# Batch 0's token-major k made by TensorE transposes, weights in 4 KB rows, constants in two loads, new order tables

## The chip, the cores and the metric

One core of a Trainium2 chip runs the whole program. The metric is device time in microseconds (us). Three executions of the kernel before took 506.56, 507.03 and 507.12 us; the median, 507.03, is the time before.

## The reference

Per batch (8 of them, 576 tokens) a retention layer feeds a gated MLP with spatial mixing:

```python
scores = (q @ k.T) / sqrt(64)                    # 8 heads of 64
D[t, s] = gamma_h ** (t - s) if t >= s else 0    # gamma_h = 1 - 2 ** (-5 - h)
x = concat_heads((scores * D) @ v)               # 576 x 512
h = relu(x @ w_in)                               # w_in 512 x 1024
u, v = h[:, :512], h[:, 512:]
v_n = (v - mean(v)) / sqrt(var(v) + 1e-6)        # over the 512 features
v_s = w_spatial @ v_n + b_spatial[:, None]       # over the 576 tokens
out = (u * v_s) @ w_out                          # w_out 512 x 512
```

Weights come in as float64, all other inputs as float32.

## The kernel before

**Tiling.** A batch is four chunks of 128 tokens and a tail of 64. The retention is computed chunk by chunk as small fp32 products of 64x64: scores inside a chunk, a running state (k times v, decayed) from chunk to chunk, and the state's share of the output. They are written to two PSUM tiles called `r` in the listings. Everything after the retention is done in wide products: each fp32 value is split into a high and a low part (`split_quarter`, `weight`, `spatial`), and a product is three products of parts (`mm3`), written to four PSUM banks called `m`. The projection by the u half of w_in and the output projection of batches 2 to 7 use sums and differences of quarter blocks (`made_weight`, `summed_quarter`, `product_chain`), seven block products in place of eight.

**The state of a chunk.** `update` multiplies the token-major k (tile `kn`) by v (`vv`), so k must stand in two layouts: feature-major for the scores (the second half of tile `qk`) and token-major for the state. Before, both come by DMA (`load`), and `prep_k` scales the token-major one by a decay per token. `state_chain` holds the update, the half state `sh`, the decays `dec` and the new state `st`. `burst_chain` adds the state's share to the output in two halves (`carried`, each 16 small products for a chunk), between which ScalarE writes a 1x2 copy (`turned`, called the turn copy below); then come `values` and the evacuation.

**Weights.** `fetch` loads 512 KB of a float64 weight as 32-bit words, and `weight` turns them into a high and a low part: GpSimd or VectorE masks the sign word (the tiles `lent_vn` and `f`), ScalarE moves it to a bank (m<-lent_slot), VectorE puts the fraction in (two operations), ScalarE casts the high part (win<-lent_vn), and GpSimd or VectorE subtracts for the low part (win<-lent_vn,win). In the listings `lent_slot` holds the v half of w_in, `raw` the u half.

**The order.** All engines run in program order. Each step is a generator, and a table of tokens says whose next stage is issued: `g.1.2` is the next stage of the scores of batch 1, chunk 2; `b` is a burst, `p` a state chain, `k` and `q` the scaling of k and q, `w` a weight, `d` the loads of a chunk, `W` a block product, `K`, `R`, `Z`, `Y` the splits of its right sides; letters behind the numbers choose the engine. `ORDER` holds the start and batches 0 and 1, `STEADY` is run four times for one batch after another, `LAST` ends the program, and the digits of `BANKS` give the PSUM bank of each product in turn. A token `z` issues a product on a zeroed tile (`wsp`, 128x512) whose result is not used; the text calls it a spin:

```python
def spin(name, n):
    ps = bank()
    for i in range(n):
        pe.matmul(ps, idle[:, :P], idle, start=True, stop=True)
```

All loads are issued by SyncE (SP) in the order of the tokens, and land through 16 DMA engines.

Of the kernel before, what the change touches and what calls it, by code (L numbers as in the profile page):

```python
# [18 lines left out]
P = 128  # L19
# [24 lines left out]
    d.0.0 d.0.0 c.a q.0.0.p d.0.0 z.22.1 k.0.0.v z.4.1 z.0.1 z.12.1 z.26.1 z.36.1 z.27.1 z.17.1 z.18.1 z.29.1  # L44
    z.10.1 z.6.1 z.13.1 z.16.1 g.0.0 p.0.0.va p.0.0.va z.34.1 b.0.0 z.40.1 z.21.1 z.1.1 g.0.0 D.1.0 D.1.1 p.0.0.va
    p.0.0.va w.1.0.vp w.1.0.vp w.1.0.vp w.1.1.vp b.0.0 w.1.1.vp d.0.1 d.0.1 d.0.1 p.0.0.va z.35.1 b.0.0 b.0.0
    z.14.1 z.8.1 z.3.1 z.2.1 z.30.1 b.0.0 z.20.1 z.5.1 z.39.1 k.0.1.p g.0.1 q.0.1.p D.1.2 D.1.3 d.0.2 w.1.2.pp
    w.1.1.vp w.1.0.vp b.0.0 w.1.1.vp w.1.1.vp p.0.1.aa p.0.1.aa b.0.1 w.1.3.vp p.0.1.aa b.0.1 w.1.0.vp w.1.2.pp
    w.1.3.vp w.1.1.vp w.1.0.vp g.0.1 z.25.1 z.9.1 z.41.1 z.33.1 z.31.1 z.7.1 z.28.1 b.0.1 b.0.1 z.24.1 z.38.1
    z.37.1 v.0.0 z.32.1 b.0.1 D.0.1 T.0 D.0.0 w.1.2.pp w.1.3.vp w.1.3.vp w.1.2.pp p.0.1.aa k.0.2.a w.1.2.pp g.0.2  # L50
    p.0.2.aa q.0.2.p w.1.2.pp w.1.3.vp p.0.1.aa b.0.1 w.0.1.vp g.0.2 p.0.2.aa w.0.0.vp w.0.0.vp p.0.2.aa p.0.2.aa
    w.1.3.vp z.19.1 v.0.0 z.23.1 v.0.0 b.0.2 b.0.2 v.0.0 w.0.1.vp d.0.3 q.0.3.p t.0.p t.0.p b.0.2 d.1.0 b.0.2 v.0.0
    p.0.2.aa b.0.2 w.0.1.vp w.0.1.vp c.t D.0.2 S d.1.0 d.1.0 d.1.1 S S S w.0.2.pp k.1.0.p m q.1.0.p g.0.3 k.0.3.a
    v.0.1 z.42.1 z.11.1 v.0.1 z.15.1 v.0.1 p.0.3.ap w.0.0.vp b.0.2 w.0.0.vp v.0.0 v.0.2 v.0.2 v.0.1 t.0.p p.0.3.ap
    v.0.0 w.0.2.pp s.0.p p.0.3.ap w.0.0.vp v.0.1 w.0.2.pp g.0.3 p.0.3.ap w.0.2.pp v.0.0 b.0.3 g.1.0 b.0.3 p.1.0.pp
# [36 lines left out]
"""
STEADY = """
    W.a.0.1.C W.a.0.0.A W.a.0.0.C W.a.0.0.A W.a.0.1.A T.b W.a.0.0.A k.b.1.v W.a.0.0.C b.b.0 g.b.1 b.b.0 W.a.0.0.A
    b.b.0 W.a.0.1.A b.b.0 d.b.2 W.a.0.1.C p.b.1.vp q.b.1.p d.b.2 W.a.0.0.A d.b.2 g.b.1 p.b.1.vp W.a.0.0.B W.a.0.0.A
    p.b.1.vp b.b.0 W.a.0.0.E W.a.0.0.B v.a.4 p.b.1.vp W.a.0.0.E W.a.0.0.B v.a.0.v W.a.0.1.A W.a.0.0.B v.a.0.v
    k.b.2.p v.a.2.a W.a.0.1.B W.a.0.1.A v.a.2.a v.a.4 v.a.0.v p.b.1.vp W.a.0.1.E v.a.0.v v.a.2.a W.a.0.1.A v.a.2.a
    b.b.1 W.a.0.1.A g.b.2 W.a.0.1.B b.b.1 v.a.0.v p.b.2.pp b.b.1 v.a.0.v b.b.1 d.b.3 W.a.0.1.E W.a.0.1.B d.b.3
    p.b.2.pp v.a.1.a d.b.3 g.b.2 p.b.2.pp W.a.1.0.A v.a.1.a q.b.2.p v.a.4 W.a.1.0.A W.a.0.1.B v.a.4 b.b.1 p.b.2.pp
    W.a.1.0.A v.a.4 p.b.2.pp W.a.1.0.C v.a.4 W.a.1.0.A v.a.1.a W.a.1.0.A W.a.1.0.C k.b.3.p v.a.4 v.a.1.a W.a.1.1.C  # L100
    v.a.2.a v.a.4 W.a.1.1.A v.a.1.a v.a.3.p v.a.2.a b.b.2 g.b.3 v.a.1.a b.b.2 v.a.4 t.b.p p.b.3.vp v.a.4 t.b.p
    W.a.1.0.A b.b.2 q.b.3.p W.a.1.1.A b.b.2 d.c.0 W.a.1.1.C W.a.1.0.B d.c.0 b.b.2 v.a.4 W.a.1.1.A W.a.1.0.B v.a.4
    v.a.3.p W.a.1.0.E W.a.1.1.A v.a.4 v.a.3.p W.a.1.0.B W.a.1.0.E v.a.3.p W.a.1.1.A W.a.1.1.B W.a.1.0.B v.a.3.p
    W.a.1.1.E v.a.3.p X.a.0.0 W.a.1.1.A W.a.1.1.B p.b.3.vp W.a.1.1.E p.b.3.vp X.a.0.2 g.b.3 t.b.p p.b.3.vp X.a.0.0
    X.a.0.1 b.b.3 X.a.0.1 g.c.0 X.a.0.2 b.b.3 b.b.3 b.b.3 d.c.1 d.c.1 X.a.1.3 e.b.v d.c.0 b.b.3 Y.a.1.v e.b.v
# [929 lines left out]
```

## Time and profile before

| | before |
|---|---|
| median of three runs | 507.03 us (506.56 to 507.12) |
| the profiled execution, its own time | 506.91 us |
| its span in the trace | 504.8 us |
| granted TensorE clock, mean | 1.00 |
| TensorE (PE) busy | 498.3 us, 99% |
| VectorE (DVE) busy | 389.2 us, 77% |
| ScalarE (ACT) busy | 259.2 us, 51% |
| GpSimd (POOL) busy | 152.5 us, 30% |
| DMA | 55.52 MB, mean 110 GB/s |

The span runs from the first to the last thing that the profiler sees; the execution's own time is 2.1 us longer. PEld is TensorE's loading of stationary operands, beside its products. An engine is busy when an instruction of it runs; the time that it waits is not counted. All three vector engines have free time on average, so what is read below is where in the span TensorE waits, and for which of them.

### The profile page before, as it was taken

Reading aid. Unit: us, or ns where it says so; the run is one execution under the profiler, and the core shown is the slowest. Engines: PE = TensorE matmul, PEld = TensorE weight load, DVE = VectorE, ACT = ScalarE, POOL = GpSimd, SP = SyncE. Lnnn points to the kernel's source line nnn. Section 1 sums busy time; section 2 is a strip of 40 time slices with the busy share of each in tenths; the row PEclk is TensorE's granted clock in tenths of the full one; section 3 lists DMA queues with packets and bytes.
Section 4 is the critical chain, followed back from the end, with each engine's and each line's share of the span. In section 5 each row is a group of like instructions: output and inputs, shape, how many; then the busy total and the mean of one; then the engine's idle time right before and its main releaser. Section 6 shows DMA issues by size and latency. Waiting matters only on the chain.

```text
span 504.8 us, 17011 instructions
## 1 busy us (share of the span) xinstructions
PE 498.3 (99%) x7335; PEld 472.8 (94%) x7335; DVE 389.2 (77%) x869; ACT 259.2 (51%) x587; POOL 152.5 (30%) x133
## 2 busy tenths in 40 slices
PE   8999999999999999999999999999999999999997
PEld 6688999999999999999999999999999999999997
DVE  3787798875899876888679786888867886788756
ACT  3788535654363642647236472446525574357513
POOL 1778733252137421335014250243303240020000
PEclk9999999999999999999999999999999999999999
DMA  8979340332426322153122442054221520011002
GB/s 283 410 260 316 113 142 3 96 112 95 121 65 189 127 66 84 57 176 94 63 79 92 150 141 80 6 162 148 72 86 41 186 91 3 1 36 59 1 2 94
DMA packets 29516, 55.52 MB, mean 110 GB/s; under 512 B 2945, under 2 KB 15361, under 8 KB 29186
## 3 DMA queue, kind: packets, MB, share of 16 engines
q1 hardware_dynamic: 29442, 54.45, 32.6%
q8 instruction: 57, 0.93, 0.8%
q14 instruction: 17, 0.14, 0.1%
HBM read 45.00 MB, written 9.44 MB: 108 GB/s over the span
## 4 chain that ended last, share of the span: by engine, by line
PE 92%; DVE 4%; DMA 3%; ACT 1%; issue 0%; SPq 0%
PE m L203 78%; PE r L203 13%; DVE u L203 2%; DMA lent_slot<-in_w_in 2%; DMA fixed_terms<-in_terms 1%; DVE slot L203 1%; ACT slot L203 1%; DVE lent_vn L203 0%; DVE m L203 0%; SPq L203 0%; DVE st L203 0%; DVE at L203 0%
## 5 line engine op out<-in xcount | busy, mean ns | idle before, releaser
L203 PE MATMUL m<-wsp,vn 128*128 128x288 f32 x768 | 113.8, 297 | 0.0
L203 PEld LDWEIGHTS m<-wsp,vn 128*128 128x128 f32 x768 | 105.7, 188 | 0.7
L203 DVE TENSOR_TENSOR u<-m,u 128x288 f32<-128x288 f32 (+1 forms) x132 | 57.2, 438 | 17.2 <-PE m L203 9.8
L203 ACT COPY u<-m 128x288 f32<-128x288 f32 (+1 forms) x92 | 34.6, 384 | 33.2 <-PE m L203 24.4
L203 PE MATMUL m<-slot,win 128*128 128x288 f32 x336 | 50.5, 296 | 0.0
L203 PEld LDWEIGHTS m<-slot,win 128*128 128x128 f32 x336 | 46.7, 188 | 0.8 <-ACT u L203 0.2
L203 DVE SCALAR_TENSOR_TENSOR u<-u,m 128x288 f32<-128x288 f32 x48 | 21.2, 451 | 25.3 <-PE m L203 25.1
L203 PE MATMUL m<-slot,wout 128*128 128x288 f32 x264 | 39.8, 296 | 0.0
L203 POOL TENSOR_TENSOR slot<-u,slot 128x576 fp32r<-128x576 f32 x7 | 10.0, 1432 | 93.2 <-ACT slot L203 93.2
L203 PEld LDWEIGHTS m<-slot,wout 128*128 128x128 f32 x264 | 36.5, 188 | 0.6 <-DVE vn L203 0.3
L203 PE MATMUL m<-win,slot 128*128 128x512 f32 (+1 forms) x168 | 37.0, 351 | 0.0
L203 ACT CAST slot<-u 128x576 fp32r<-128x576 f32 x32 | 21.5, 675 | 25.6 <-DVE u L203 25.4
L203 PEld LDWEIGHTS m<-win,slot 128*128 128x128 f32 x168 | 26.7, 188 | 4.7 <-DVE slot L203 0.4
L203 ACT CAST places<-u 128x576 fp32r<-128x576 f32 x21 | 14.2, 677 | 30.5 <-DVE u L203 30.3
L203 PE MATMUL m<-quarter,slot 128*128 128x256 f32 x216 | 29.7, 283 | 0.0
L203 ACT COPY r<-warm 1x2 f32<-1x2 f32 x32 | 4.9, 152 | 47.8 <-PE r L203 47.6
L203 DVE TENSOR_TENSOR at<-r,fixed_terms 128x512 f32<-128x512 f32 x32 | 21.9, 683 | 8.5 <-PE r L203 6.9
L203 POOL TENSOR_TENSOR kn<-kn,fixed_terms 128x512 f32<-128x512 f32 x15 | 16.1, 1075 | 39.3 <-DMA kn<-in_qkv 34.1
L203 POOL TENSOR_TENSOR places<-x,places 128x576 fp32r<-128x576 f32 x6 | 10.5, 1756 | 57.0 <-ACT places L203 55.3
L203 PE MATMUL m<-slot,part 128*128 128x288 f32 x168 | 27.3, 301 | 0.4
L203 PE MATMUL m<-wtl,vt 128*128 128x288 f32 (+1 forms) x128 | 27.4, 295 | 0.0
L203 PEld LDWEIGHTS m<-quarter,slot 128*128 128x128 f32 x216 | 26.9, 188 | 0.4
(164 smaller groups left out, 1214.4 us busy)
## 6 DMA issues: line engine op xcount, KB each, us to landing
qk<-in_qkv SPq DMA_DIRECT2D x30, 512.0 KB, 4.3
kn<-in_qkv SPq DMA_DIRECT2D x30, 256.0 KB, 4.8
vv<-in_qkv SPq DMA_DIRECT2D x30, 256.0 KB, 4.7
out<-u SPq DMA_DIRECT2D x28, 144.0 KB, 1.8
tail<-in_tails SPq DMA_DIRECT2D x8, 384.0 KB, 3.5
out<-o SPq DMA_DIRECT2D x18, 144.0 KB, 1.9
lent_slot<-in_w_in SPq DMA_DIRECT2D x4, 512.0 KB, 9.3
raw<-in_w_in SPq DMA_DIRECT2D x4, 512.0 KB, 11.2
```

The source lines that it names most:

```text
L203: ins = op(*args, **kw)
```

## The change

**Token-major k of batch 0.** Chunks 0 to 3 of batch 0 no longer load `kn`. `prep_k` has two stages for them: four transposes on TensorE (`pe.transpose`, 128x128 each, by an identity tile `eye`) from the feature-major k into a bank `m`, and the scaling out of that bank into the same tile. The chunk's array in memory is laid q, k, v, k so that chunks 2 and 3, which load in one DMA, can leave it out. Batches 1 to 7 load both as before.

**Weights in 4 KB rows.** The host lays the u half of w_in and w_out so that each 512 KB load is 128 rows of 4 KB; before, a row was four pieces of 1 KB. The v half had 4 KB rows before and keeps them.

**Constants in two loads.** `terms` is cut into the mask with the decays (128x524) and the scales of q (`qterms`, 128x256); the identity (`unit`, 128x128) is a third small load. The last rows of the spatial weights come in one load in place of two.

**The tables.** ORDER, STEADY, LAST and BANKS are laid anew: the same stages with other engines for some, in another order. A few places of it follow.

SP's queue of loads at the start, before (`in_w_in` is w_in, its v half first):

```order
L203 DMA qk_94<-in_qkv 128x1024
L203 DMA kn_95<-in_qkv 128x512
L203 DMA fixed_terms<-in_terms 128x780
L203 DMA vv_96<-in_qkv 128x512
L203 DMA lent_slot_93<-in_w_in 128x512 x2
L203 DMA qk_171<-in_qkv 128x1024
L203 DMA kn_172<-in_qkv 128x512
L203 DMA vv_173<-in_qkv 128x512
L203 DMA lent_slot_93<-in_w_in 128x512 x2
L203 DMA u<-in_qkv 128x2048
```

and now (`in_w_v` is that v half):

```order
L206 DMA qk_95<-in_qkv 128x1024
L206 DMA eye<-in_unit 128x128
L206 DMA fixed_terms<-in_terms 128x524
L206 DMA vv_97<-in_qkv 128x512
L206 DMA qk_118<-in_qkv 128x1024
L206 DMA qs<-in_qterms 128x256
L206 DMA lent_slot_94<-in_w_v 128x512
L206 DMA vv_120<-in_qkv 128x512
L206 DMA u<-in_qkv 128x1536
L206 DMA lent_slot_94<-in_w_v 128x512 x3
L206 DMA lent_wout_136<-in_qkv 128x1536
```

Chunk 1's q and k moved ahead of all weights, both chunks' `kn` loads are gone, and three of the four v weights moved behind chunk 2 (`u`).

ScalarE at the start, before:

```order
L203 CAST slot_207<-r_90 128x2x4x64
L203 CAST win_66<-lent_vn_92 128x512
L203 ACTIVATE dec_79<-sh,fixed_terms 128x64 x4
L203 COPY r_90<-warm 1x2
L203 CAST win_66<-lent_vn_92 128x512
L203 ACTIVATE m_87<-lent_slot_93 128x512
L203 ACTIVATE m_86<-lent_slot_93 128x512
L203 CAST slot_207<-r_90 128x2x4x64
L203 ACTIVATE u<-u,fixed_terms 128x64 x8
```

and now:

```order
L206 CAST slot_263<-r_91 128x2x4x64
L206 ACTIVATE dec_80<-sh,fixed_terms 128x64 x4
L206 ACTIVATE u<-m_90,fixed_terms 128x64 x8
L206 COPY r_91<-warm 1x2
L206 CAST win_67<-lent_vn_93 128x512
L206 ACTIVATE m_90<-lent_slot_94 128x512
L206 ACTIVATE dec_79<-st_76,fixed_terms 128x64 x4
L206 ACTIVATE m_87<-lent_slot_94 128x512
L206 CAST win_67<-lent_vn_93 128x512
```

The scaling of chunk 2's k (u, x8, now out of the bank `m_90`) moved ahead of the first weight's casts (win<-lent_vn), and the moves of weights 0 and 2 to their banks stand behind it.

VectorE in a steady batch, around the gating (SCALAR_TENSOR_TENSOR on `u`) and the splits behind it (u<-u is a difference of quarter blocks, slot<-u,slot and places<-u,places the low part of a quarter), before:

```order
L203 TENSOR_TENSOR slot_831<-u,slot_831 128x2x288
L203 SCALAR_TENSOR_TENSOR u<-u,m_86 128x288
L203 SCALAR_TENSOR_TENSOR u<-u,m_89 128x288
L203 TENSOR_TENSOR u<-u 128x2x288 x3
L203 TENSOR_TENSOR places_2105<-u,places_2105 128x2x288
L203 TENSOR_TENSOR slot_831<-u,slot_831 128x2x288
L203 TENSOR_TENSOR u<-u 128x2x288
L203 TENSOR_TENSOR o_1481<-m_88,o_1481 128x288
```

and now:

```order
L206 SCALAR_TENSOR_TENSOR u<-u,m_88 128x288
L206 TENSOR_TENSOR u<-u 128x2x288
L206 TENSOR_TENSOR slot_944<-u,slot_944 128x2x288
L206 TENSOR_TENSOR u<-m_90,u 128x288
L206 TENSOR_TENSOR u<-u 128x2x288
L206 SCALAR_TENSOR_TENSOR u<-u,m_87 128x288
L206 TENSOR_TENSOR slot_944<-u,slot_944 128x2x288 x2
L206 TENSOR_TENSOR xt<-r_91,xt 128x4x64
L206 TENSOR_TENSOR x_1116<-xt 128x8x32
L206 TENSOR_TENSOR u<-u 128x2x288
```

Before, three differences stand between the last gating and the next low part of `slot`; now they stand ahead of it, and two low parts follow right behind it.

The diff, with a line or two of each table:

```diff
-    d.0.0 d.0.0 c.a q.0.0.p d.0.0 z.22.1 k.0.0.v z.4.1 z.0.1 z.12.1 z.26.1 z.36.1 z.27.1 z.17.1 z.18.1 z.29.1
+    d.0.0 z.26.1 z.21.1 z.27.1 z.20.1 z.0.1 z.18.1 z.29.1 z.38.1 z.36.1 z.5.1 z.1.1 z.24.1 z.13.1 z.11.1 z.22.1 c.e
+    c.a d.0.0 d.0.1 c.q D.1.1 d.0.1 q.0.0.p m q.0.1.p d.0.2 D.1.3 D.1.0 D.1.2 d.0.3 T.0 D.0.0 k.0.0.v z.2.1 g.0.0
...
-    W.a.0.1.C W.a.0.0.A W.a.0.0.C W.a.0.0.A W.a.0.1.A T.b W.a.0.0.A k.b.1.v W.a.0.0.C b.b.0 g.b.1 b.b.0 W.a.0.0.A
+    W.a.0.1.A W.a.0.0.A T.b k.b.1.v W.a.0.0.A v.a.4 v.a.4 v.a.4 W.a.0.0.C W.a.0.0.C W.a.0.1.A W.a.0.0.A W.a.0.1.A
...
-    fixed_terms = cp.tile([P, 2 * NP * D + NP * D + H + NP], F32, name="fixed_terms")
+    fixed_terms = cp.tile([P, 2 * NP * D + H + NP], F32, name="fixed_terms")
     am = fixed_terms[:, :512].rearrange("r (i p n) -> r i p n", i=2, p=NP)
-    qs = fixed_terms[:, 512:768].rearrange("r (p n) -> r p n", p=NP)
-    kd = fixed_terms[:, 768:768 + H].rearrange("r (h n) -> r h n", n=1)
-    sd = fixed_terms[:, 768 + H:].rearrange("r (p n) -> r p n", n=1)
+    kd = fixed_terms[:, 512:512 + H].rearrange("r (h n) -> r h n", n=1)
+    sd = fixed_terms[:, 512 + H:].rearrange("r (p n) -> r p n", n=1)
+    qs = cp.tile([P, NP, D], F32, name="qs")
...
+    def eye():
+        return keep("eye", [P, P], tag="o1")
...
-            qk, kn, vv = t[:, :2], t[:, 2], t[:, 3]
+            qk, vv, kn = t[:, :2], t[:, 2], t[:, 3]
...
-            parts = (qk, qkv[b, c, :, :2]), (kn, qkv[b, c, :, 2]), (vv, qkv[b, c, :, 3])
-        else:
-            parts = (t, qkv[b, c]),
+            parts = (qk, qkv[b, c, :, :2]), (kn, qkv[b, c, :, 3]), (vv, qkv[b, c, :, 2])
+            parts = parts if b else parts[::2]
+        else:
+            parts = (t[:, :3], qkv[b, c, :, :3]),
...
-            dma(t.bitcast(U64), w_in[i * P:(i + 1) * P, DH:])
         else:
             t = keep("raw", [P, NCB * S], I32)[:, i * 1024:(i + 1) * 1024] if i < 2 else keep(f"raw{i}", [P, 1024], I32)
-            w = w_in if kind == 0 else w_out
-            dma(t.bitcast(U64).rearrange("p (a n) -> p a n", a=NCB), w[:, i * P:(i + 1) * P].rearrange("(a p) n -> p a n", p=P))
+        dma(t.bitcast(U64), (w_u, w_v, w_out)[kind][i])
...
     def prep_k(b, c, eng=po):
         kh = chunk[b, c][2].rearrange("p (h d) -> p h d", h=H)
-        scale(kh, kh, kd, eng)
+        if b:
+            scale(kh, kh, kd, eng)
+            yield
+            return
+        ps = bank()
+        for p in range(NP):
+            pe.transpose(ps[:, p * P:(p + 1) * P], chunk[b, c][1][:, p], eye())
+        yield
+        scale(kh, ps.rearrange("p (h d) -> p h d", h=H), kd, eng)
...
-        for i in range(2):
-            dma(w[i * TL:(i + 1) * TL, NC], w_sp[NC * P:, :])
+        dma(w[:, NC], w_sp[NC * P:, :])
...
-        "c": lambda k: dma_one(*{"a": (fixed_terms, terms), "t": (amt, tmask)}[k]),
+        "c": lambda k: dma_one(*{"a": (fixed_terms, terms), "q": (qs, qterms), "e": (eye(), unit), "t": (amt, tmask)}[k]),
...
-        "k": lambda b, c, how: once(prep_k, int(b), int(c), on(how)),
+        "k": lambda b, c, how: prep_k(int(b), int(c), on(how)),
...
-    terms = np.concatenate([a.reshape(P, -1) for a in (am, qscale, kdec, per ** D)], axis=1)
-    return {"terms": f(terms), "tmask": f(amt)}
+    terms = np.concatenate([a.reshape(P, -1) for a in (am, kdec, per ** D)], axis=1)
+    return {"terms": f(terms), "qterms": f(qscale), "unit": f(np.eye(P)), "tmask": f(amt)}
...
+    def cut(a):
+        return c(a.reshape(4, P, 4, P).transpose(2, 1, 0, 3).reshape(4, P, 512)).view(np.uint64)
+
+    w_in = moe_w_in.reshape(H, D, -1)[[0, 1, 3, 2, 4, 5, 7, 6]].reshape(H * D, -1)
...
-        "qkv": c(np.stack([fc(qf), fc(kf), tkc(kn), tkc(vv)], axis=3)),
+        "qkv": c(np.stack([fc(qf), fc(kf), tkc(vv), tkc(kn)], axis=3)),
...
-        "w_in": c(moe_w_in.reshape(H, D, -1)[[0, 1, 3, 2, 4, 5, 7, 6]].reshape(H * D, -1)).view(np.uint64),
-        "w_sp": c(moe_w_spatial.T[:, _PLACES]),
+        "w_u": cut(w_in[:, :DH]),
+        "w_v": c(w_in[:, DH:]).view(np.uint64).reshape(NCB, P, DH),
+        "w_sp": c(np.concatenate([w_sp, w_sp[m:]])),
         "b_sp": c(moe_b_spatial.reshape(1, S)[:, _PLACES]),
-        "w_out": c(moe_w_out).view(np.uint64),
+        "w_out": cut(moe_w_out),
```

## Rows read from the trace of the kernel before

**Rows 1.** The page, part 1: busy time, share of the span, instructions.

```profile
PE 498.3 (99%) x7335; PEld 472.8 (94%) x7335; DVE 389.2 (77%) x869; ACT 259.2 (51%) x587; POOL 152.5 (30%) x133
```

**Rows 2.** Stretches: us, busy us of PE, PEld, DVE, ACT, POOL; clock; DMA share, GB/s.

```profile
0.00:10.00 10.00, 8.35 (x88) 6.14 (x89) 1.88 (x6) 2.48 (x5) 1.44 (x5) 1.00 0.82 267
10.00:20.00 10.00, 8.92 (x188) 6.63 (x189) 7.33 (x15) 5.73 (x18) 5.69 (x5) 1.00 1.02 394
20.00:30.00 10.00, 9.90 (x203) 7.35 (x202) 8.66 (x16) 10.00 (x35) 7.03 (x7) 1.00 1.04 405
...
40.00:50.00 10.00, 10.00 (x159) 8.81 (x157) 7.13 (x22) 8.55 (x20) 8.86 (x9) 1.00 0.98 323
```

**Rows 3.** Timeline, PE, the start: start, us, operation, count, [idle before, releaser].

```profile
1.50 6.32 PE L203 MATMUL m<-wsp 128*128 128x512 f32 x14 [1.50 <-DVE wsp L203]
...
33.83 0.27 PE L203 MATMUL r<-qsc,sh 64*64 64x64 f32 x1
...
34.37 0.68 PE L203 MATMUL r<-qk 64*64 64x64 f32 x32
34.83 0.68 PE L203 MATMUL r<-vv,kn 64*64 64x64 f32 x32
...
37.98 2.00 PE L203 MATMUL m<-win,xt 128*128 128x512 f32 x8
39.81 1.35 PE L203 MATMUL m<-slot,win 128*128 128x288 f32 x9
```

**Rows 4.** Timeline, PE, around one group of small products.

```profile
233.70 0.96 PE L203 MATMUL m<-slot,win 128*128 128x288 f32 x6
234.50 1.74 PE L203 MATMUL m<-places,win 128*128 128x288 f32 x12
236.17 0.27 PE L203 MATMUL r<-qk,sh 64*64 64x64 f32 x1
...
238.43 1.85 PE L203 MATMUL m<-slot,quarter 128*128 128x288 f32 x12
```

**Rows 5.** Timeline, PE and PEld, the wait of a steady batch.

```profile
265.26 0.95 PE L203 MATMUL m<-slot,wout 128*128 128x288 f32 x6
266.17 0.19 PEld L203 LDWEIGHTS m<-slot,part 128*128 128x128 f32 x1 [0.19 <-ACT o L203]
...
266.67 1.49 PEld L203 LDWEIGHTS m<-slot,part 128*128 128x128 f32 x11 [0.31 <-DVE slot L203]
...
384.97 0.19 PEld L203 LDWEIGHTS m<-slot,part 128*128 128x128 f32 x1 [0.18 <-ACT o L203]
```

**Rows 6.** Timeline, DVE, the last v weight.

```profile
17.77 0.64 DVE L203 TENSOR_SCALAR lent_vn<-lent_slot 128x512 int32<-128x512 int32 x1 [1.92 <-DMA lent_slot<-in_w_in]
```

**Rows 7.** Timeline, ACT and POOL, the start.

```profile
14.95 0.62 ACT L203 CAST win<-lent_vn 128x512 fp32r<-128x512 f32 x1 [1.60 <-DVE lent_vn L203]
15.88 1.06 ACT L203 ACTIVATE dec<-sh,fixed_terms 128x64 f32<-128x64 f32 x4 [0.31 <-DVE sh L203]
16.59 1.54 POOL L203 TENSOR_SCALAR lent_vn<-lent_slot 128x512 f32<-128x512 f32 x1 [0.75 <-DMA lent_slot<-in_w_in]
...
17.45 1.19 ACT L203 ACTIVATE m<-lent_slot 128x512 f32<-128x512 f32 x2
18.10 2.70 POOL L203 TENSOR_TENSOR win<-lent_vn,win 128x512 fp32r<-128x512 f32 x2
...
20.36 2.02 ACT L203 ACTIVATE u<-u,fixed_terms 128x64 f32<-128x64 f32 x8
```

**Rows 8.** The page, part 5: group, count, busy and mean, idle before, releaser.

```profile
L203 ACT COPY r<-warm 1x2 f32<-1x2 f32 x32 | 4.9, 152 | 47.8 <-PE r L203 47.6
```

**Rows 9.** Chain of waits, the part ahead of the steady wait: start, us, what.

```profile
262.27 0.47 DVE u L203
...
265.14 0.69 ACT slot L203
...
265.85 0.77 DVE slot L203
```

More of the change, by code (lines that the diff above doesn't have):

```diff
@@ new lines @@
+    V.0.2 V.0.0 V.0.2 V.1.2 V.1.0 T.1 D.0.2 w.0.2.pp d.1.2 w.0.3.pv D.2.1 w.2.0.vv d.1.3 d.1.3 d.1.3 b.1.0 V.0.1
+    w.0.2.pp V.0.0 b.1.0 k.1.2.p b.1.1 w.2.0.vv w.2.0.vv w.2.0.vv p.1.1.pp w.0.2.pp w.0.2.pp w.0.3.pv b.1.1
+    w.0.2.pp V.1.2 p.1.2.pa b.1.1 b.1.1 g.1.2 G.0.1 w.0.2.pp w.0.3.pv w.2.1.vp w.0.3.pv k.1.3.p V.1.1 V.1.1
+    p.1.1.pp p.1.2.pa p.1.2.pa G.1.2 G.0.1 V.1.0 V.1.3 G.0.2 w.2.1.vp b.1.1 p.1.2.pa w.2.1.vp w.2.1.vp G.1.2 g.1.2
+    w.2.1.vp w.0.3.pv V.1.3 w.2.0.vv D.2.2 w.0.3.pv w.2.2.vv b.1.1 A.0.0.v q.1.3.p q.1.2.p d.2.0 d.2.0 A.0.1.p
@@ new lines @@
+    t.1.p v.1.0 G.1.1 A.0.5.v G.1.1 A.0.2.v V.0.3 b.1.2 p.1.3.pp g.1.3 w.2.0.vv A.0.6.v A.0.9.v w.2.2.vv b.1.2
+    t.1.p b.1.2 b.1.2 V.0.3 b.1.2 p.1.2.pa g.1.3 A.0.12.v A.0.13.v w.2.2.vv G.0.2 g.2.0 d.2.1 d.2.1 D.2.3 d.2.0
+    v.1.0 v.1.0 v.1.0 G.1.3 G.0.3 A.0.3 v.1.0 p.1.3.pp w.2.2.vv p.1.3.pp v.1.0 b.1.2 G.1.3 t.1.p p.1.3.pp v.1.0
+    k.2.0.v v.1.0 P.1.1.v v.1.2 b.1.3 p.2.0.vp P.1.0.v b.1.3 P.0.0.p A.0.7 b.1.3 b.1.3 v.1.2 v.1.1 v.1.1 v.1.1
+    v.1.1 G.0.3 P.1.1.v e.1.v e.1.v A.0.4.v v.1.0 e.1.v A.1.1.v P.1.0.v v.1.0 y.1.0.0 v.1.2 v.1.2 v.1.4 b.1.3
@@ new lines @@
+    b.b.1 W.a.0.1.B W.a.0.1.E v.a.2.a v.a.0.v b.b.1 v.a.2.a v.a.2.a W.a.0.1.C t.b.p k.b.2.p p.b.2.pp p.b.1.vp
+    p.b.2.pp p.b.2.pp b.b.1 W.a.0.1.B W.a.1.0.A W.a.1.0.C v.a.0.v v.a.2.a v.a.0.v v.a.1.a W.a.1.0.A W.a.1.0.A
+    W.a.1.0.A W.a.0.1.B v.a.2.a v.a.3.p p.b.2.pp p.b.2.pp q.b.2.p v.a.1.a W.a.1.0.C g.b.2 v.a.1.a W.a.1.0.B
+    W.a.1.0.A W.a.1.0.A b.b.1 d.b.3 d.b.3 d.b.3 W.a.1.1.A W.a.1.1.C v.a.1.a v.a.3.p v.a.1.a v.a.1.a W.a.1.0.B b.b.2
+    b.b.2 g.b.3 k.b.3.p q.b.3.p t.b.p p.b.3.vp b.b.2 b.b.2 W.a.1.1.A v.a.3.p v.a.4 v.a.4 W.a.1.1.C v.a.4 v.a.4
@@ new lines @@
+    p.b.3.vp X.a.1.0 b.b.3 W.a.1.1.B X.a.1.0 b.b.3 Y.a.1.v X.a.1.1 W.a.1.1.B X.a.1.1 Y.a.1.v Z.a.5.vv b.b.3 b.b.3
+    e.b.v e.b.v X.a.1.2 e.b.v Z.a.5.vv R.b.1.v X.a.1.3 X.a.1.3 Z.a.7.vv W.a.2.0.A X.a.0.3 X.a.0.2 Y.a.3.v b.b.3
+    Y.a.3.v Z.a.5.vv Z.a.7.vv Z.a.7.vv X.a.0.3 Z.a.6.vv X.a.0.2 W.a.2.0.A Z.a.6.vv Y.a.2.v R.b.1.v K.b.5.vv
+    Z.a.6.vv Y.a.2.v Z.a.4.vv W.a.2.0.D W.a.2.1.A W.a.2.0.D W.a.2.1.D W.a.2.1.D W.a.2.1.A Z.a.4.vv R.b.2.v
+    W.a.2.1.B W.a.2.0.A W.a.2.0.A W.a.2.1.A W.a.2.0.B W.a.2.1.A K.b.7.vv Z.a.4.vv W.a.2.0.A R.b.3.p W.a.2.0.A
@@ new lines @@
+    W.a.2.1.A R.b.3.p K.b.6.pv W.a.2.1.A W.a.2.0.B W.a.2.0.B W.a.2.0.B W.a.2.1.C W.a.2.1.C W.a.2.1.B W.a.2.1.B
+    W.a.2.1.B W.a.2.1.B W.a.2.0.B W.a.2.0.C W.b.0.0.A R.b.2.v W.a.2.0.C W.a.2.0.C W.a.2.1.E W.a.2.1.E W.a.2.1.C
+    W.a.2.1.E W.b.0.1.A W.a.2.0.E K.b.5.vv K.b.7.vv K.b.6.pv K.b.6.pv K.b.4.vv W.a.2.0.E W.b.0.0.A W.b.0.1.A
+    K.b.7.vv W.b.0.0.A K.b.4.vv W.b.0.0.A W.b.0.0.C W.b.0.1.A K.b.5.vv W.b.0.0.C W.b.0.0.A W.b.0.0.B K.b.4.vv
+    W.b.0.0.E W.a.2.0.E W.b.0.0.A W.b.0.0.B W.b.0.0.E v.b.0.v v.b.0.v W.b.0.1.A v.b.0.v W.b.0.1.C W.b.0.0.B
@@ L153, in retention_gmlp @@
 @with_exitstack
-def retention_gmlp(ctx, tc, qkv, tails, w_in, w_sp, b_sp, w_out, terms, tmask, out):
+def retention_gmlp(ctx, tc, qkv, tails, w_u, w_v, w_sp, b_sp, w_out, terms, qterms, unit, tmask, out):
     nc = tc.nc
@@ L465, in prep_k @@
         kh = chunk[b, c][2].rearrange("p (h d) -> p h d", h=H)
-        scale(kh, kh, kd, eng)
+        if b:
[7 more added lines that the diff above has]
+        scale(kh, ps.rearrange("p (h d) -> p h d", h=H), kd, eng)
+        yield
     def prep_tail(b, eng=po):
```

175 lines of the change are left out of this document (75 added, 100 removed).

## The prediction

> **What bounds the kernel now.** I read the busy shares first. TensorE (PE) is busy 99% of the 504.8 us span [rows 1]. So only three things can move the end: what PE is given, the time it waits, and the head and tail in which it has nothing to do. The stretches come next [rows 2]: the DMA queues are full from 10 to 30 us, and PE is at 8.35 and 8.92 of 10 us in the first two stretches and at 9.90 in the third. Some of that is not work: 43 products on a zeroed tile ("spins") stand in the order to keep PE going until data are there, 14 of them ahead of the first real product.
>
> The PE timeline of the start gives prices [rows 3]. The 14 opening spins take 6.32 us, 0.45 each, while later 512-wide products step at (39.81 - 37.98)/8 = 0.23. The granted clock reads 1.00 for both [rows 2]; by their steps the opening ones run at the lower level (1.2 GHz) and the later ones at the higher (2.4 GHz). Both kernels open on the same spins with nothing before them, so this cancels. A 64x64 product steps at (34.83 - 34.37)/16 = 0.029 (each has two records).
>
> Further on, PE changes between wide products and groups of small ones. Around one group [rows 4]: 288-wide products step at (234.50 - 233.70)/6 = 0.133, so the twelve from 234.50 should free PE at 236.10, and the group starts at 236.17; its 72 small products take 2.26 where 72 x 0.029 is 2.09; the twelve after it take 1.85 where the twelve before took 1.74. That is about 0.35 us for a group. The built programs have 46 groups before and 42 after.
>
> There is one plain wait in a steady batch [rows 5]: six products start at 265.26 and should free PE at 266.06, but the next one, the first on `part`, starts at 266.17 and the second at 266.67, held by a ScalarE copy and then by VectorE's low part of `slot`. That is 0.11 + 0.37 = 0.48 us. It stands in each of the four steady batches; the last has it at 384.97, two batches of 59.4 us later. Otherwise PE hardly waits after 30 us.
>
> **The change part by part.** Sums are against the profiled execution, 506.91 us (the span and 2.1 around it), which is 0.12 under the median of 507.03.
>
> Spins and real products are the same in number. PE gains 16 transposes of 128x128, which no row shows. By width, one would be half of a 256-wide product, and that steps no slower than its 288-wide neighbours: 0.06. From above, the small fp32 products: if four of them run at once in four quarters of the array, one takes 4 x 0.029 for 64 columns, and 128 columns take 0.24. I take 0.12, between the two and nearer the wide products: 1.9 us in all, bounds 1.0 and 3.8.
>
> The Trainium skill ("TensorE: Matmul & The Clock Gate", Part 4: PE-mode transpose) gives about 275 ns for a bf16 transpose of this size inside one kernel, and says that transposes don't raise the clock as products do. No run here shows either yet. By 0.275 each, the sum below would lose 1.9 us more.
>
> *Loads.* In the queue, chunk 1's q and k move ahead of all weights, chunks 2 and 3 lose their 256 KB of token-major k, and the four v weights fall back. Bytes moved: 2.67 MB by 10 us, then 0.394 MB/us [rows 2]. Before, the last v weight is 4.59 MB deep in the queue and is waited for until 17.77 [rows 6], when 5.73 MB had moved: 1.1 MB of later transfers went along. With the same 1.1 on top, chunk 2 (3.35 MB deep now) lands at 14.5, v weight 0 (4.40) at 17.2, weight 2, the last (4.92), at 18.5, chunk 3 (5.71) at 20.4. The v weights are complete 0.8 us later than before, the chunks several us earlier.
>
> *The start.* Ahead of its first v product PE now has 41 spins, 16 transposes and 152 small products: 7.9 (the first 15 spins) + 26 x 0.23 + 16 x 0.12 + 152 x 0.029 + 5 x 0.35 = 22.0 us without waits. ScalarE decides whether it waits. By the same steps chunk 1's state products end at 13.9, and 0.4 of VectorE later its half state is there. From 14.5 on ScalarE's order is: cast 0.6, decay 1.06, eight scalings of chunk 2's k 2.02, turn copy 0.15, cast 0.6, move 0.6, decay 1.06, move 0.6, cast 0.6 [rows 7, 8]: the high part of v weight 0 is there at 21.8. GpSimd subtracts for the first weight from 18.9 (1.35), masks another (1.54) and then makes weight 0's low part (1.35), at 23.2. So the second v product waits until 23.3, 1.1 us. Eleven products (2.5) lead to 25.8, the next group, of 72, to 28.4 with 0.1 for the turn copy, a spin and a product to 28.9, weight 2's low part (two casts, two subtractions) to 29.3, and twenty products to 34.0.
>
> There PE has done 33 v products, 224 small ones and 42 spins. Before, it had done 30, 224 and 43 at 33.83 [rows 3]. So 34.0 - 33.83 - 3 x 0.23 + 0.23 = **-0.3 us**, transposes included: the lighter loads pay for the transposes and little more. VectorE takes chunk 1's k over from GpSimd, some 0.7 (its 0.77 for the wider tile [rows 9]); it is busy 7.33 of 10 us there [rows 2], which covers it; uncovered it is 0.7.
>
> *After the start.* 36 groups of small products are left against 37: **-0.35**.
>
> *Steady batches.* Before, the awaited low part needs, behind PE's last gated product, the gating 0.47, three differences as long as a low part, a cast 0.69 and the low part 0.77 on the chain [rows 9]: 4.2 and the hand-overs. PE had 16 small and 24 wide products and one change for it: 0.5 + 3.2 + 0.35 = 4.0. In the new order two of the differences stand ahead of the last gating, and the low parts follow right behind it: 0.47 + 0.69 + 2 x 0.77 = 2.7, while PE has 72 small and 12 wide products to pass, 4.0. The wait goes: 4 x 0.48 = **-1.9**. What is late next there is a ScalarE copy between two products in one bank, with six products (0.80) as its cover.
>
> *At nothing.* The weights' 4 KB rows: in the stretch from 40 us, with 1 KB rows, the queues move 323 GB/s at a share of 0.98, against 405 from 20 to 30 [rows 2]; a weight of 512 KB would land 0.3 us sooner. PE is at 10.00 of 10 us there and waits for none of them; without that cover it is a gain of up to 0.3 for each of eight. The constants in two loads and one load fewer for the spatial weights lie under the same work; uncovered, a load is as long as its bytes, 0.3.
>
> Sum: -0.3 - 0.35 - 1.9 = -2.55: 504.4 for the profiled execution, **504.5** against the median.
>
> **Rivals.** *Slow transposes.* At 0.24 each, the twelve ahead of ScalarE's chain push all that follows by 12 x 0.12 = 1.4: 505.9. For it: that chain has no slack until weight 2's low part. Against: every full-height product in the trace steps far below that. At the skill's 0.275 it would be 506.4.
>
> *The steady wait only moves.* If the bank copies take its place, -0.65 is left: 506.4. For it: 0.11 of the old wait is such a copy [rows 5]. Against: that copy was late because a cast stood before it on ScalarE.
>
> *Slower: the turn copy.* In each of 32 bursts PE stops between two halves until ScalarE has written one 1x2 copy. The new tables draw the steps of a burst together, mostly with 16 small products (0.47) between the halves. If in the 51% of the time that ScalarE is busy [rows 1] the copy comes half a cast (0.31) later than its cover lasts, that is 32 x 0.51 x 0.31 = 5.1 us: 509.6. From a mean wait of 0.08 on it eats the whole gain, from 0.11 it is measurable as slower. Against: ScalarE waited 47.6 us in all for PE ahead of these copies [rows 8], so it is mostly ready first.
>
> **How the numbers follow.** The forecast holds with a chance of 0.71, slow transposes 0.10, the moved wait 0.09, the turn copy 0.10. A change within 0.2%, 1.0 us, is about what the measurement can't tell from none. Faster (below 506.0): the forecast and nearly half of the first rival, 0.75; the rest of it and the second, 0.15; slower 0.10. The range: the bounds of the transposes (12 x 0.06 below, 12 x 0.12 above) with 1.5 us either way for the landings give 502.3 to 506.5 for the forecast's own; up to 507.2 it takes in the first two rivals and leaves out the third.
>
> **What would show it.** The first v product on a low part near 23.3 us and batch 0's last scores before 28; transposes that step near 0.12; no wait on `part` in the steady batches, which repeat after 58.9 instead of 59.4 us. Wrong would be: transposes above 0.2; a PE held by ScalarE between the halves of many bursts; or a first v product after 26 us, where the start alone eats the steady gain.

## The result, and the profile after

The change made the kernel slower. Twenty executions took a median of 511.91 us (507.10 to 513.64) against 506.68 for twenty of the kernel before; the ratio is 1.0086, with a 95% interval of 1.0071 to 1.0101. The profiled execution took 510.2 us, 3.3 more than that of before; its span is 508.4.

The page, part 1 (busy us, share, instructions), answers to [rows 1]:

```profile
PE 496.1 (98%) x7351; PEld 473.9 (93%) x7351; DVE 397.4 (78%) x870; ACT 259.1 (51%) x587; POOL 156.4 (31%) x132
```

PE does 2.2 us less and stands idle for 12.3 us of its span where it was 6.5. Where, the stretches say (to be read beside [rows 2]):

```profile
0.00:10.00 10.00, 7.88 (x86) 5.98 (x86) 1.96 (x5) 1.63 (x3) 0.20 (x4) 1.00 0.81 246
10.00:20.00 10.00, 9.96 (x237) 8.01 (x238) 6.70 (x14) 7.59 (x28) 4.84 (x6) 1.00 1.00 407
20.00:30.00 10.00, 7.12 (x166) 5.40 (x169) 5.06 (x10) 7.53 (x24) 8.26 (x7) 1.00 0.88 284
```

From 10 to 20 us PE is better filled than before (9.96 against 8.92), and from 20 to 30 it loses 2.9 us. The list of PE's waits (engine, tile, what it waited for: us in all, times, longest) names the cause of the longest "issue": PE waited for nothing that the profile shows.

```profile
PE r L206 <- issue: 4.2, 3, 2.5
...
PE r L206 <- ACT r L206: 1.2, 2, 1.0
PE m L206 <- issue: 0.7, 1, 0.7
```

The PE timeline (start, us, operation, count, [idle before, releaser]) shows these stops between two products of one step, inside bursts or just behind one:

```profile
10.04 0.66 PE L206 MATMUL m<-eye,qk 128*128 128x128 f32 x4 [0.31 <-DMA qk<-in_qkv]
10.46 1.86 PE L206 MATMUL m<-wsp 128*128 128x512 f32 x7
...
21.26 0.56 PE L206 MATMUL r<-at,vv 64*64 64x64 f32 x19
22.20 0.45 PE L206 MATMUL r<-at,vv 64*64 64x64 f32 x13 [0.38 <-issue]
22.58 3.05 PE L206 MATMUL m<-win,slot 128*128 128x512 f32 x12
...
27.07 0.22 PE L206 MATMUL r<-qsc,st 64*64 64x64 f32 x1
29.79 0.21 PE L206 MATMUL r<-qsc,sh 64*64 64x64 f32 x1 [2.50 <-issue]
...
206.28 1.85 PE L206 MATMUL m<-places,wout 128*128 128x288 f32 x12
207.97 0.95 PE L206 MATMUL m<-slot,part 128*128 128x288 f32 x6
...
265.22 1.85 PE L206 MATMUL m<-places,wout 128*128 128x288 f32 x12
...
300.87 0.52 PE L206 MATMUL r<-at,vv 64*64 64x64 f32 x20
302.76 0.45 PE L206 MATMUL r<-at,vv 64*64 64x64 f32 x12 [1.37 <-issue]
```

Against the step of the products around them, four such stops cost 0.58 us (21.60), 2.70 (27.07), 1.57 (301.17) and 0.83 (411.93), 5.7 in all. The kernel before has none. In the steady batches the wait on `part` is gone (207.97 carries no bracket, and no product or weight load on `part` waits 0.1 us or more), and a batch repeats after 265.22 - 206.28 = 58.94 us.

**What the stops have in common** came from counting. A record of PE is two instructions, a weight load and a product; with one for each instruction of the program that only waits, the next instruction after each stop has these numbers:

| stop at | records of PE before it | instruction | modulo 256 |
|---|---|---|---|
| 21.60 | 348 | 705 | 193 |
| 27.07 | 475 | 961 | 193 |
| 301.17 | 4801 | 9666 | 194 |
| 411.93 | 6455 | 12993 | 193 |

The page, part 3 (DMA queue: packets, MB, share), has a queue that moves instructions:

```profile
q8 instruction: 57, 0.93, 0.8%
```

That is 16 KB a packet; 57 x 256 is 14,592 of PE's 14,793 instructions. The packets that end before the four stops do so at 20.87, 28.39, 301.33 and 411.61 us, and PE goes on 1.3 to 1.4 us after each. The Trainium skill ("Runtime: NRT & Kernel Launch", Instruction fetch mechanics) states that an engine's instructions are fetched in blocks of 256, which agrees, and that an engine issues more slowly than they come in, so that fetching is hidden. The stops would have to have another cause by that. The experiments below asked which it is; they go against this last statement, and the measurement decides.

### The profile page after: what moved, and what is told of

It reads as the page before. It is cut to its first block, busy times and chain, and to the rows that moved or that the text cites. A ratio compares the mean times of both kernels' runs of the same rounds, so it can differ in the third digit from the quotient of the medians.

```text
span 508.4 us, 17086 instructions
## 1 busy us (share of the span) xinstructions
PE 496.1 (98%) x7351; PEld 473.9 (93%) x7351; DVE 397.4 (78%) x870; ACT 259.1 (51%) x587; POOL 156.4 (31%) x132
## 4 chain that ended last, share of the span: by engine, by line
PE 89%; ACT 3%; DVE 3%; DMA 2%; issue 2%; SPq 0%; ACTq 0%; DVEq 0%
PE m L206 76%; PE r L206 14%; DMA qk<-in_qkv 1%; ACT m L206 1%; DMA out<-o 1%; DVE part L206 0%; ACT wsp L206 0%; SPq L206 0%; DVE quarter L206 0%; DVE u L206 0%; ACT vn L206 0%; DVE x L206 0%; ACT wtl L206 0%; ACT win L206 0%; ACT vl L206 0%
## 5 line engine op out<-in xcount | busy, mean ns | idle before, releaser
L206 PE MATMUL m<-wsp,vn 128*128 128x288 f32 x768 | 112.2, 295 | 0.5 <-DVE vn L206 0.5
L206 POOL TENSOR_TENSOR slot<-u,slot 128x576 fp32r<-128x576 f32 x7 | 11.3, 1617 | 102.4 <-ACT slot L206 102.4
L206 PE MATMUL m<-slot,wout 128*128 128x288 f32 x264 | 38.7, 295 | 0.0
L206 PE MATMUL m<-win,slot 128*128 128x512 f32 (+1 forms) x168 | 34.8, 348 | 0.4 <-ACT o L206 0.4
L206 PE MATMUL m<-wtl,vt 128*128 128x288 f32 (+1 forms) x128 | 27.3, 296 | 0.0
L206 PE MATMUL m<-slot,part 128*128 128x288 f32 x168 | 26.0, 296 | 0.0
L206 PE MATMUL m<-places,wout 128*128 128x288 f32 x168 | 25.7, 297 | 0.0
L206 POOL TENSOR_TENSOR qk<-qk,qs 128x512 f32<-128x512 f32 (+1 forms) x16 | 20.4, 1276 | 12.0 <-PE r L206 8.6
L206 ACT CAST slot<-x 128x576 fp32r<-128x576 f32 x24 | 15.4, 674 | 16.8 <-POOL x L206 14.6
```

The lines of the kernel that those rows point to most:

```text
L206: ins = op(*args, **kw)
```

## The experiments

**Moving the borders.** The theory: PE uses its instructions up in blocks of 256 and stands still at a border when the next block has not come. The rival: each stop belongs to what the order makes late there (a load, a turn copy, a transpose). Instructions added at the very start tell them apart, since they move the borders and leave the order as it is:

```diff
+    def pad(n):
+        w = idle.bitcast(F32)
+        for _ in range(n):
+            pe.matmul(bank_tiles[3][:D, :D], w[:D, :D], w[:D, D:2 * D], start=True, stop=True)
+        yield
...
-    d.0.0 z.26.1 z.21.1 z.27.1 z.20.1
+    d.0.0 x.11 z.27.1 z.20.1
```

(`x.11` is `pad(11)`: 44 instructions, less 4 for two spins.) Three kernels had it. The small products take longer than the spins that they replace, so the first real product also starts later: at 8.55 us for 6.58 in the first of the three, at 15.28 in the second, and at 8.34 for 7.75 in the third.

> The changed kernel with 11 small products on the zeroed tile in place of 2 opening spins: 40 instructions more ahead of everything, nothing else moved. Theory (TensorE's instructions arrive in blocks of 256, and it stands still at a block's border when it has used a block up before the next has come): every border lies 40 instructions, some 20 product records, earlier in the work. The stall of 2.7 us at 27.07 moves ahead of the last 20 records of its burst and shrinks to 0.5 to 2, those at 301.2 and 411.9 leave their places, one appears near 241 us; 506 to 509 us. Rival (the stalls belong to what the order makes late: a turn copy, a load, a transpose): the same stalls between the same products, 509.5 to 512 us.

Measured: 508.75 us (1.0039, 1.0024 to 1.0054). The stops at 27.07, 301 and 411 are gone; at borders stand 0.91 at 14.97, 0.54 at 85.11 and 1.28 at 241.88 us. The last was expected there, the first two were not. That at 27.07 was expected to shrink, not to go, and the shift is not all that took it away: the queues carried 0.00 MB from 21 to 23.2 us in this run, and the block came at 24.73 us, 1.5 after the border before it, where it came 5.2 after in the changed kernel (more on its queues below).

> The changed kernel with 47 small products in place of 6 opening spins: 176 instructions more ahead of everything. Theory (blocks): the stall leaves 27.07 for 32 us (about 5 us there), another of some 1.4 near 363, none at 301.2 and 411.9; 509 to 514 us, and above the run with 40 instructions by 2 us or more. Rival (order): the same stalls between the same products as in the changed kernel, within 1 us of it.

Measured: 519.07 us (1.024, 1.0209 to 1.0271). No stop at 301 or 411; 3.30 at 35.26 and 1.32 at 370.45, at the borders expected (the first was priced at 5). The total is 5 us over its range: the 47 opening products were slower than the spins that they replaced, and spins still stepped at 0.43 us, the lower level, at 14 us. So this run shows places, not a price.

> The kernel before with 11 small products in place of 2 opening spins: 40 instructions more ahead of everything. Theory (blocks): a kernel that had no such stall gets some by the shift alone, near 29.7, 132, 148 and 303 us; 508 to 511 us, slower than before by 1.5 to 4. Rival (order): no stall in the middle of a burst, within 0.5 us of before.

Measured: 513.32 us (1.0129, 1.0095 to 1.0164), 2 us above the range. The kernel before, which had no such stop, gets four, 0.48 at 15.41, 1.21 at 28.05, 0.89 at 132.47 and 0.72 at 148.78; three of the four places were expected, and the one expected near 303 did not come. The view puts the last down to VectorE, but PE goes on there 1.3 us after a packet, as at the others. Another 2 us are waits for ScalarE and VectorE at 43.8 and 158.2, which come after stops; whether they come by them was not traced. Its PE timeline:

```profile
27.75 0.51 PE L200 MATMUL r<-lent_wout 64*64 64x64 f32 x19
29.27 0.45 PE L200 MATMUL r<-lent_wout 64*64 64x64 f32 x13 [1.01 <-issue]
...
132.23 0.53 PE L200 MATMUL m<-slot,win 128*128 128x288 f32 x2
133.49 0.80 PE L200 MATMUL m<-slot,win 128*128 128x288 f32 x4 [0.73 <-issue]
```

The stop at 28.05 follows record 475, as the one at 27.07 in the changed kernel does, with other products on both sides of it. In all seventeen traces 40 waits of PE over 0.3 us are called issue, and 39 of them stand at instruction 193 or 194 modulo 256 (the other, of 0.36 us, is at 165.92 us in `after_mend3` below). Counted by the step, 44 products at such a border start 0.4 us or more after the one before. Each of the 44 starts 1.2 to 1.6 us after the end of the packet of its number, the first packet being that of the second border; and of 966 borders none was passed sooner than 1.2 us after that. The rival falls.

With the same 40 instructions ahead, measured together, the changed kernel (508.75 us) is 4.6 us faster than the kernel before (513.32). So which of the two is faster depends on such a shift.

**Which tables lose.** The tables were crossed; the same stages stand in both.

> The kernel before with the new tables for the steady and last batches alone. Prediction's step: the wait of 0.48 us goes in each of four steady batches, 1.9 us in all: 504.8 us without stalls at block borders, and a steady batch repeats after 58.9 us instead of 59.4. Theory (blocks): the same, but the borders lie elsewhere, so up to 2.5 us of stalls may come back: 504.5 to 507.5, each us above 504.8 found at a border. Rival (the steady gain is not real): 506.4 or more with no stall at a border.

Measured: 507.56 us (1.0010, 0.9995 to 1.0024); the span of its profiled execution is 504.1, 0.7 less than before. No wait on `part`; one stop of 0.66 at a border, at 298.97, and longer waits for a k (0.78 at 13.97) and a v (0.44 at 51.70). The steady gain is there in the trace and not in the median: the profiled execution, 505.84 us, is the second fastest of ten, and why the median lies 1.7 us above it was not traced.

> The new table of the start with the old tables for the steady and last batches. The waits of 0.48 us in each of four steady batches come back (1.9 us); the stalls at 21.6, 27.07 and the turn copy's at 132.88 stay. Theory (blocks): those at 301.2 and 411.9 (2.4 us) leave, and others come where the old batches have bursts: 509 to 512 us, and waits on `part` by name in the trace. Rival (the new steady tables lose by themselves what the kernel lost): 507 us or less.

Measured: 511.65 us (1.0093, 1.0068 to 1.0118). The four waits on `part` are back, the stop at 411 is gone and that at 301 is 0.30. The new steady tables are not what lost.

**Why a block is late.** At 22.20 PE passes a border and has, by the theory, asked for the block it lacks at 27.07. Two stretches of the DMA view (queue, kind: packets, MB, share) of the changed kernel, 22.2 to 27.3 us and 27.3 to 28.5:

```profile
q1 hardware_dynamic: 532, 1.56, 96.9%
...
q1 hardware_dynamic: 146, 0.45, 95.8%
q8 instruction: 1, 0.02, 5.1%
```

For 5 us the queues carry loads alone; then the block comes, and 1.4 us later PE goes on. At 301, with quiet queues, PE goes on 302.76 - 299.21 = 3.55 us after the border before. The next kernel holds the loads back, since the fourth part of the spatial weights lies where the third v weight is read last:

```diff
     def dma_wsp():
...
-        for sb in range(NC):
+        for sb in (3, 2, 1, 0):
             dma(w[:, sb], w_sp[sb * P:(sb + 1) * P, :])
```

> The changed kernel with the four loads of spatial weights in the order 3, 2, 1, 0 in place of 0, 1, 2, 3. The first of them has to wait until the third v weight has been read (about 24.8 us), and SP's later loads wait behind it, so the DMA queues are empty from 22 to 25 us. TensorE's instruction stream is the same, block by block. Theory (the block asked for at 22.2 us waits behind 5 us of queued loads): it comes at about 25.5, the stall of 2.70 us at 27.07 is gone, that at 21.6 stays; 506.5 to 508.5 us. Rival (the block itself is slow to come, whatever is queued, or the stall has another cause): 2 us or more are left at the same border; 509.5 to 512 us.

Measured: 513.95 us (1.0133, 1.0118 to 1.0148), a miss in the total. The same view of this kernel, 22.3 to 23.9 us and 23.9 to 25.2:

```profile
q1 hardware_dynamic: 3, 0.01, 1.3%
...
q8 instruction: 1, 0.02, 5.3%
```

With nothing queued the block comes 3.4 us sooner, and the stop at 27.07 is gone: that much is shown. The other traces agree. In the seven kernels that hold loads and in the two shifted ones with the new start, whose queues are near empty at that border, this block begins 1.1 to 1.7 us after the border before; in the five with loads queued, 3.9 to 5.9. In the kernel before the queues are as full (103.8% from 24.05 to 26.35 us), and yet the block begins 2.3 us after its border. Whether the new order of the loads or the 4 KB rows make that difference, no run tested.

But PE then waits 4.60 us at 31.46, because VectorE waits for a weight that stood behind the held loads:

```profile
35.21 0.43 DVE L206 TENSOR_SCALAR f<-raw 128x512 int32<-128x512 int32 x1 [5.59 <-DMA raw<-in_w_u]
```

Then the second u weight was put first (`D.0.1 S d.1.0 S d.1.1` in place of `S d.1.0 S d.1.1 D.0.1`):

> The changed kernel with the loads of spatial weights in the order 3, 2, 1, 0, as in the run that held them, and the load of the second u weight (raw) moved ahead of the first of them: what VectorE waited for there comes first, and the queues still run empty before 25 us. TensorE's instructions are the same. Theory (the block waits behind queued loads): the block asked for at 22.2 us comes by 26, no stall at 27.07 and no wait at 31.5, TensorE's clock stays up; 506.5 to 508.5 us. Rival (a held load always costs what the stall did, since some engine needs it): a wait of 2 us or more between 25 and 45 us; 510 us or more.

Measured: 511.53 us (1.0088, 1.0069 to 1.0107). The rival of that expectation holds: no stop at 27.07, and 3.1 us of waits at 34 and 36 us, for the tail's mask and batch 1's first k:

```profile
34.98 0.42 DVE L204 TENSOR_TENSOR att<-r,amt 128x256 f32<-128x256 f32 x1 [1.86 <-DMA amt<-in_tmask]
```

And then the mask, and that chunk's loads together (`D.0.1 c.t S d.1.0 d.1.0 d.1.0 S d.1.1`):

> The changed kernel with its loads behind 20 us in the order in which they are needed: the second u weight, the tail's mask, then the hold (spatial weights in the order 3, 2, 1, 0), then q, k and v of batch 1's first chunk together, the other spatial weights behind them. TensorE's instructions are the same. Theory (the block asked for at 22.2 us waits behind queued loads, and the waits of 3.1 us at 33 to 36 us in the second holding run came from the mask and that chunk's k alone): no stall at 27.07, under 0.5 us of waits between 28 and 45; 506.5 to 508.5 us. Rival (the start is bound by its loads, and what the block gains some load loses): 2 us or more of waits between 28 and 45, 510 us or more.

Measured: 510.43 us (1.0095, 1.0065 to 1.0125), its rival again. Its profiled execution, 514.47 us, is the slowest of its four by 4, so the sizes here may not be typical. Now a cast of spatial weights ahead of a turn copy is late, and PE waits 3.23 us at 34.55:

```profile
34.45 0.67 ACT L204 CAST wsp<-lent_slot 128x576 fp32r<-128x576 f32 x1 [2.12 <-DMA lent_slot<-in_w_sp]
```

Three orders of loads, and each time something waits for what was held: in none of them do the loads up to about 36 us leave a gap to give away. Whether a fourth order does better stays open.

**Filling the stop.** If PE waits at 27.07 for its block alone, work put ahead of it costs nothing (`x.10` is here ten spins):

```diff
-            pe.matmul(bank_tiles[3][:D, :D], w[:D, :D], w[:D, D:2 * D], start=True, stop=True)
+            pe.matmul(bank_tiles[banks[0]], idle[:, :P], idle, start=True, stop=True)
...
-    q.0.2.p b.0.2 g.0.3
+    q.0.2.p b.0.2 x.10 g.0.3
```

> The changed kernel with 10 spins (2.3 us at the higher clock) in the burst at 25.8 us, ahead of the stalled border; later borders fall 20 instructions earlier in the work. Theory (PE waits there for its next block, which comes at a time of its own): the spins fit into the stall, which shrinks from 2.70 to 0.5 or less, the clock doesn't fall behind it, and the median, in which the clock mostly fell, goes down by 1 to 3 us: 508 to 511 us in spite of 2.3 us more work. Rival (the stall is a wait for another engine's work that starts when PE gets there, or the border is not its cause): the spins are added to it; 513 us or more.

Measured: 509.70 us (1.0055, 1.0039 to 1.0072), 2.2 less than the changed kernel with 2.3 us more work on PE; by the ratios, each to the kernel before on its own chip, it is 1.6 less. The stop at 27 is gone (two stand at later borders, 1.20 at 242.27 and 1.79 at 301.59):

```profile
25.89 2.56 PE L204 MATMUL m<-wsp 128*128 128x512 f32 x10
28.39 1.16 PE L204 MATMUL r<-lent_wout 64*64 64x64 f32 x64
29.37 0.41 PE L204 MATMUL r<-tail 64*64 64x64 f32 x16
...
29.84 0.65 PE L204 MATMUL r<-at,u 64*64 64x64 f32 x32
```

It also points to why the median of the changed kernel lies 1.7 us above its profiled execution. Of its 20 executions 14 had a mean granted clock of 0.997 or less, with a median of 512.3, the other six 509.8; with the spins all six had 0.999 or more. What happens behind a long stop is seen in the profile of the run on the turn copy (below), whose stop at that border was 3.15 us (columns as in [rows 2]):

```profile
27.00:31.00 4.00, 1.06 (x71) 0.92 (x67) 0.00 (x0) 1.20 (x4) 2.68 (x3) 1.00 1.03 390
31.00:35.00 4.00, 4.00 (x45) 3.21 (x36) 3.78 (x7) 2.08 (x6) 1.04 (x1) 0.57 0.61 197
```

After the stop the granted clock is 0.57 for 4 us: PE's products go at the lower of its two levels (1.2 against 2.4 GHz) for most of it. The stop costs its own length and, where the clock falls, this. That it falls at this place in the 14 executions is likely and not shown, since only one execution of each kernel is profiled.

**The turn copy.** In the profile after, ScalarE's row ahead of the longest wait of that kind (timeline):

```profile
133.31 0.67 ACT L206 CAST places<-u 128x576 fp32r<-128x576 f32 x1 [1.77 <-DVE part L206]
133.89 0.15 ACT L206 COPY r<-warm 1x2 f32<-1x2 f32 x1
```

```diff
-    A.2.3 A.2.4.v Y.1.1.v b.2.1 g.2.2
+    A.2.3 A.2.4.v b.2.1 Y.1.1.v g.2.2
```

> The changed kernel with one token moved: in the burst at 132 us the turn copy stands ahead of ScalarE's cast of a quarter block, which waits for a low part of VectorE in memory that both share; before this it stood behind. TensorE's instructions stay at their places. Theory (the prediction's third rival at this one place): the wait of 1.19 us at 132.88 goes, all else stays: 1 to 1.2 us less than the changed kernel. Rival (PE would wait for the sum of k and v or for the scores there anyway): 0.3 us or less.

Measured: 510.72 us (1.0072, 1.0052 to 1.0091), 1.2 less than the changed kernel, though on another chip, and with ratios whose intervals overlap. In the trace the wait is gone and the cast stands behind the copy:

```profile
133.73 0.15 ACT L204 COPY r<-warm 1x2 f32<-1x2 f32 x1 [0.77 <-PE r L204]
134.72 0.67 ACT L204 CAST places<-u 128x576 fp32r<-128x576 f32 x1 [0.84 <-DVE part L204]
```

**Put together.** Five kernels joined the mends. The first (`after_mend`) had the first holding order, the copy moved and 14 small products behind the burst at 134 us; 503.5 to 505.5 us were expected, and it took 513.60 (1.0114, 1.0082 to 1.0146). The stops at 301 and 411 gave way to one of 0.62 at 243.97, but the wait of the first holding run was back, 3.85 us at 31.18. The next two follow the second holding run, with the copy moved, without and with 14 small products behind the burst at 134 us:

> As the run before, and the turn copy at 132 us moved ahead of ScalarE's cast. Theory: 1.2 us less than that run, 505.3 to 507.3 us, with the stalls at 301 and 411 (2 to 2.4 us) still there.

> As the run before, and 14 small products on the zeroed tile's place behind the burst at 134 us: 56 instructions, 0.41 us. Theory (block borders): the stalls at 301 and 411 go, one of about 0.6 at 244 comes; 1 to 1.6 us less than without the products; 503.8 to 506 us, faster than both kernels. Rival (work added to TensorE costs its time): 0.4 us more than without them.

Measured: 511.40 us (1.0094, 1.0076 to 1.0112) and 511.19 (1.0095, 1.0074 to 1.0116). The stops at 299.6 and 410.3 (1.58 and 0.60) give way to one of 0.90 at 243.7, where 0.6 was expected. That is 1.3 us less of stops for 0.41 of products, but the medians differ by 0.2; the rest was not traced. Both miss their range by 4 us or more; the run that they rest on missed its by 3.

> As the run before, with the turn copy at 132 us moved and 14 small products behind the burst at 134 us. Theory: 1.2 us less by the copy, and the stalls at 301 and 411 (2.2) give way to one of 0.6 to 0.9 at 244, for 0.41 us of products: 504.3 to 506.3 us, faster than both kernels. Rival (the start is bound by its loads): 509 us or more.

Measured: 509.99 us (1.0071, 1.0056 to 1.0085): its rival, with 2.06 us of waiting for a turn copy at 34.61.

> The changed kernel with the 10 spins of the run before, the turn copy at 132 us moved, and 9 small products behind the burst at 134 us, so that the late borders fall 56 instructions earlier in the work than in the changed kernel. Loads as in the changed kernel. Theory: 1.2 us less by the copy and 2 to 2.5 less at 242 and 301 us than in the run with the spins alone, for 0.26 us of products and a stall of 0.3 near 238: 506 to 508 us, level with the kernel before. Rival (stalls come back elsewhere whatever the shift): 508.5 us or more.

Measured: 508.68 us (1.0043, 1.0028 to 1.0058), 0.7 above the range and in that of its rival. The profiled execution is at 507.73, with stops of 0.54 and 0.90 left at borders, the second where 0.3 was expected. By the ratios half of the loss is had back; no kernel here beats the one before.

## Why the prediction was wrong

It said 504.5 us with a range of 502.3 to 507.2, and 0.75 for faster; the kernel is 1% slower. By its steps:

- **What bounds the kernel.** Here it failed. It named three things that can move the end, PE's work, its waits, the head and tail, and counted as waits only those that the trace of before shows. PE's wait for its own instructions isn't among them, since that kernel has none; and that it has none is luck of its borders, for 40 instructions more give it four such stops, 3.3 us. So no term of the sum stood for it, and no rival.
- **The start.** The failing step in place: "the next group, of 72, to 28.4 with 0.1 for the turn copy". The products were priced at 0.029 each, a rate that holds only as long as the next block is there. That group began at 25.55 and ended at 30.4, with 2.70 us of standing still in it. Up to it the sum was near: the transposes step at (10.46 - 10.04)/4 = 0.105 where 0.12 was taken, so the rival of slow transposes falls (though not by the argument against it, for a 512-wide product steps at 0.23, hardly below 0.24); the first v products start at 22.58, on the low part that was forecast for 23.2. The point forecast at 34.0 came at 35.86, 3.3 of it stops: with these taken off, the start is 1.4 us better than said. That is a subtraction; in the runs that lost the long stop by holding loads, other waits took its place.
- **After the start.** -0.35 for groups was no match for what came: stops of 2.4 us at 301 and 412, and two waits of 0.54 and 0.61 (for an output's copy at 106.4 and for a low part at 116.1), which the prediction did not look for.
- **Steady batches.** Right: the four waits are gone, and a batch takes 58.94 us where 58.9 was said. Crossing the tables shows that it belongs to them.
- **The turn copy.** The third rival had the right mechanism and the wrong measure: it is late at two of 32 bursts by 1.19 and 0.37 us, 1.4 more than before, not 5.1. It said that "the new tables draw the steps of a burst together" and saw in it a danger for ScalarE's copy alone; the stops stand in bursts or just behind one, but whether the drawing together makes them was not tested apart from the shift of the borders.
- **At nothing.** The 4 KB rows and the split constants show in no wait; no run took them away, so they were not tested by themselves.

The sum, for the profiled executions: 504.4 forecast, and 5.7 at borders, 1.4 at turn copies and 1.15 in the two other waits make 512.7; the measured 510.2 is 2.5 less, of which 1.4 is the better start, and 1.1 was not traced. The median lies another 1.7 us up, where the prediction took the 0.12 of before; the likely cause is the fall of the clock behind the stop at 27 us. The range's upper end of 506.5 for the forecast's own is not the sum of its terms either (504.5 + 1.4 + 1.5 = 507.4), but the result lies outside both.

## What to carry to other kernels

Count the instructions of an engine that runs many short ones, and mark every 256th (here from the 193rd on): a block of nothing but these small products lasts 128 x 0.0147 = 1.9 us here, and the next one took about 3.5 us from border to border with quiet queues and 7.6 behind 5 us of loads. A change that adds or takes away a few instructions early moves all later borders, so a kernel with such bursts can gain or lose about 1% by it: 40 instructions took the kernel before from 507.04 to 513.32 us and the changed one from 511.91 to 508.75. Before a new order is judged, run it with two or three shifts. Other work put ahead of a late block cost nothing here as long as the block was not there: ten spins of 2.3 us fitted into the stop.

## What the runs showed of the hardware

- TensorE's instructions came in packets of 16 KB through the DMA queues, behind loads issued earlier: 3.4 us sooner where nothing was queued (24.0 for 27.4 us). At the four stops PE went on 1.3 to 1.4 us after the packet had ended, and at no border of any trace sooner than 1.2 us after.
- A dense block isn't enough for a stop: before has one that lasts 1.86 us (355.15 to 357.01), and its packet began at 354.2, ahead of the border. So it matters too how early the packet begins; what lets it begin ahead of the border was not tested.
- After a stop of 2.7 us the clock stayed up in one profile and after one of 3.15 it fell to 0.57 in another; what decides between them was not tested.
